# A float32-accurate mixture-of-experts chain on one core: second-layer weights fetched ahead of the float64 conversion and split later, and one vector instruction less per scaling round

## The chip, the cores and the metric

The kernel runs on one core of one Trainium2 chip. The metric is the device time of one execution in microseconds (us); lower is better. A difference of 0.2% here is about 4 us.

## The reference

Three layers follow each other. The first is a windowed attention with global tokens (batch 4, 8 heads, 512 local and 32 global tokens, head size 64); its output x has T = 2176 tokens of 512 numbers. The second, where the change lies, is a mixture of experts in which each token gets a weighted sum of all experts:

```python
P = np.exp(x @ w_gate - max)
for _ in range(8):
    P /= P.sum(1, keepdims=True) + 1e-09
    P /= P.sum(0, keepdims=True) + 1e-09
    P *= N / E
for e in range(E):                       # E = 8
    h = np.maximum(x @ w1[e], 0.0)       # 512 -> 1024
    out += P[:, e:e + 1] * (h @ w2[e])   # 1024 -> 512
```

The third is a dense layer, `elu(x @ w_in) @ w_out`, whose weights (512 x 2048 and 2048 x 512) come as float64.

## The kernel before

**Numbers in two pieces.** TensorE multiplies each matrix as a high and a low piece of 32-bit numbers, three matmuls per product. So each weight that is loaded is "split": ScalarE (ACT) rounds it to the high piece, and VectorE (DVE) or GpSimd (POOL) subtracts that from the weight to get the low piece.

**Phases.** The middle layer is cut into units u = 0 to 15 (half an expert each: 512 hidden columns) and into two sets of tokens, p = 0 (1024 tokens) and p = 1 (1152 tokens). Units 0 and 1 of p = 0 are computed during the attention. The other 30 pairs (p, u) are the phases of the loop at the end of the mixture, numbered a = 0 to 29: a = 0 to 13 have p = 0, a = 14 to 29 have p = 1. A phase has two parts:

- `mix1`: x @ w1, relu, by Strassen's method in its Winograd form. A "quad" (class `Quad`) makes four output blocks from seven products of six matmuls each. A quad's products come in the order 1, 6, 2, 7, 5, 4, and its product 3, which accumulates in the PSUM bank of product 5, comes later, after product 2 of the next quad (for the last quad: in mix2). For p = 0 there are 2 quads of 512 columns, for p = 1 there are 4 quads of 288 columns. Below, "q2.1" is product 1 of the third quad (q0 is the first). ACT copies product 1 out of PSUM (`s`, L834), DVE adds the others to kept sums (`u`, L836, and `t`, L822), ACT makes the relu's high piece (`hh`, L825), DVE the low piece (`hl`, L827).
- `mix2_all`: h @ w2 per tile of 128 tokens (8 tiles for p = 0, 9 for p = 1), 12 matmuls of 512 columns a tile, and DVE adds the result, scaled by P, to the sum (`acc`, L891).

The eight PSUM banks are handed out in turn, so a product or a tile gets the bank of the one eight places before it, and waits until that one has been read.

**Side work.** What else must be done is laid into two lists, `side1` and `side2`, whose items are issued a few at a time after each product of mix1 and each tile of mix2 (function `pop`; `None` is an empty place). All engines run their instructions in the order in which they are issued. The items are:

- `ld1`, `b1` (from `weights1`): two 512 KB loads `w1r` of the next phase's w1 (L669), and 18 items that form and split its Strassen sums (POOL L677, ACT L681, DVE L685).
- `ld2`, `nbuild` (from `weights2`): two 512 KB loads `w2r` of the next phase's w2 (L714), and four items that split it (ACT `w2h` L101, POOL `w2l` L105).
- `cv` (from `weights64`): one or two pieces of the third layer's float64 weights in each phase from a = 2 on (none at a = 13; two at a = 20 to 25): a load `r` of 512 KB (L728), `words` (six DVE instructions, L738 to L743), and `parts` (two on ACT, three on POOL, the last of which makes `cl`, and two stores of 256 KB, L755 and L756, of `ch` and `cl`).
- `plan` (from `sinkhorn`): the eight scaling rounds of P, begun before the loop and ended in phase 0; `cols` is the half of a round that divides by column sums.

All loads and stores are issued by SyncE (SP), in one queue in program order: an issue that waits holds up the ones behind it. The loads `w1r`, `r` and `w2r` share four buffers (`raw_tile`) that are handed out in turn.

Of the kernel before, what the change touches and what calls it, by code (L numbers as in the profile page):

```python
# [16 lines left out]
ALU = mybir.AluOpType  # L17
# [5 lines left out]
T = B * (SL + SG)  # L23
D = H * HD
E, F1 = 8, 1024
F2 = 2048
FU = 512
NT = T // 128
# [20 lines left out]
def tile_net(ctx: ExitStack, tc, kq, vw, vc, qg, wg, w1, w2, wi, wo, consts, out):  # L49
    nc = tc.nc  # L50
# [12 lines left out]
    pr = const.tile([128, NT, E], F32, tag="pr", name="pr")  # L63
# [301 lines left out]
    def put_x(ps, hi, lo):  # L365
        nc.scalar.copy(hi, ps)
        nc.vector.tensor_tensor(out=lo, in0=ps, in1=hi.bitcast(F32), op=ALU.subtract)
# [243 lines left out]
    def raw_tile(shape, dt, name):  # L611
        r = rawm.tile([128, 2 * HALF], F32, tag="raw", name=name)
        n = int(np.prod(shape))
        v = r[:, :n].bitcast(dt)
        return v.rearrange("p (a f) -> p a f", a=shape[0])
# [93 lines left out]
    def weights2(u):  # L709
        v = {}  # L710

        def load(i):
            v[i] = raw_tile((2, 512), F32, "w2r")
            nc.sync.dma_start(v[i], w2[u][:, 2 * i:2 * i + 2])  # L714

        return [lambda: load(0), lambda: load(1)], [
            lambda k=k: split(w2s["h"][:, k], w2s["l"][:, k], v[k // 2][:, k % 2]) for k in range(4)
        ]
# [41 lines left out]
    def sinkhorn():  # L760

        s = {}

        def gmax():
            mx = sm.tile([128, 1], F32, tag="mx", name="mx")
            nc.vector.tensor_reduce(out=mx, in_=lg.rearrange("p t e -> p (t e)"), axis=AX.X, op=ALU.max)
            mb = sm.tile([128, 128], F32, tag="mb", name="mb")
            nc.vector.tensor_copy(mb, mx.to_broadcast([128, 128]))
            s["mb"] = mb

        def expm():
            ps = ps2.tile([128, 512], F32, tag="n", name="pmx")
            nc.tensor.transpose(ps[:, :128], s["mb"], ident)
            nm = sm.tile([128, 1], F32, tag="nm", name="nm")
            nc.vector.tensor_reduce(out=nm, in_=ps[:, :128], axis=AX.X, op=ALU.max, negate=True)
            nc.scalar.activation(
                pr.rearrange("p t e -> p (t e)"), lg.rearrange("p t e -> p (t e)"), AF.Exp, bias=nm
            )

        def rows():  # L780
            r = sm.tile([128, NT], F32, tag="rs", name="rs")
            nc.vector.tensor_reduce(out=r, in_=pr, axis=AX.X, op=ALU.add)
            nc.vector.tensor_scalar_add(r, r, 1e-9)
            nc.vector.reciprocal(r, r)
            nc.vector.tensor_tensor(
                out=pr, in0=pr, in1=r.rearrange("p (t o) -> p t o", o=1).to_broadcast([128, NT, E]), op=ALU.mult
            )
            c = sm.tile([128, E], F32, tag="cs", name="cs")
            nc.vector.tensor_reduce(out=c, in_=pr.rearrange("p t e -> p e t"), axis=AX.X, op=ALU.add)
            s["c"] = c  # L790

        def cols():
            ps = ps2.tile([128, 512], F32, tag="n", name="pcs")
            nc.tensor.matmul(ps[:, :E], ones, s["c"], start=True, stop=True)
            r = sm.tile([128, E], F32, tag="rc", name="rc")
            nc.vector.tensor_scalar_add(r, ps[:, :E], 1e-9)
            nc.vector.reciprocal(r, r)
            nc.vector.tensor_tensor(
                out=pr, in0=pr, in1=r.rearrange("p (o e) -> p o e", o=1).to_broadcast([128, NT, E]), op=ALU.mult
            )  # L800
            nc.vector.tensor_scalar_mul(pr, pr, float(T) / E)

        return [gmax, None, expm] + [rows, None, cols] * 8

# [88 lines left out]
    side1, side2 = deque(), deque()  # L893

    def pop(q, n=1):
        for _ in range(n):
            if q:
                f = q.popleft()
                if f is not None:
                    f()  # L900
# [40 lines left out]
    with tc.manual_schedule():  # L941
        conv = deque(range(8 * U2))
        plan, sums = sinkhorn(), sums_of_x(0, SL)[1]
        first, build = weights1(2)

        pre, plan = deque(sums[:-2] + first + build[:9]), deque(plan)
        steps = 0
        for r in fill:
            steps += 1
            if steps % 4 == 0:  # L950
                pop(pre)
            if steps % 8 == 0:
                pop(plan)
        pop(pre, len(pre))
        for f in build[9:13]:
            f()
        order = [(0, u) for u in range(2, U1)] + [(1, u) for u in range(U1)]
        nload, nbuild = weights2(2)
        side1.extend(build[13:] + sums[-2:] + nload)
        for a, (p, u) in enumerate(order):  # L960
            after = order[a + 1] if a + 1 < len(order) else None
            switch = after is not None and after[0] != p
            if a > 0:
                side1.extendleft(reversed(nbuild))
            else:
                side1.extend(nbuild)
            cv = []
            if after is not None:
                ld1, b1 = weights1(after[1])
                ld2, nbuild = weights2(after[1])  # L970
                side1.extend(ld1)
                if not switch:
                    for _ in range(min(len(conv), 0 if a < 2 else 2 if 19 < a < 26 else 1)):
                        cv.append(weights64(conv.popleft()))
                    side1.extend(ld for ld, _ in cv)
            if a == 0:

                rest, n = list(side1), len(plan)
                side1.clear()
                for b in range(n):  # L980
                    side1.extend(rest[b * len(rest) // n:(b + 1) * len(rest) // n])
                    side1.append(plan.popleft())
            last = mix1(p, u)
            pop(side1, len(side1))
            if after is None:
                break
            if switch:
                ldx, sums = sums_of_x(1, HALF)

                for f in ldx[4:]:  # L990
                    f()
                b1 = ldx[:4] + [f for pair in zip(b1, sums[:12]) for f in pair] + b1[12:] + sums[12:14]
                nbuild = sums[14:] + nbuild
            side2.extend(b1)
            for _, ops in cv:
                side2.extend(ops)
            side2.extend(ld2)
            mix2_all(p, u, last)
            pop(side2, len(side2))
            if switch:  # L1000
                for i in range(TP[0] // 128):
                    nc.sync.dma_start(yd[:, i], accs[i])


        mleft.close()
        fin = ctx.enter_context(tc.tile_pool(name="fin", bufs=1, side="left", reuse_waits="tile"))
        raws = ctx.enter_context(tc.tile_pool(name="raws", bufs=2, side="left", reuse_waits="tile"))
        xh = fin.tile([128, 4, T], F32R, tag="xh", name="xh")
        xl = fin.tile([128, 4, T], F32R, tag="xl", name="xl")
        wset = [{n: fin.tile([128, 4, 512], F32R, tag=s + n, name=s + n) for n in ("1h", "1l")} for s in "AB"]  # L1010

        def x2_t(i, src):
            ps = ps2.tile([128, 4, 128], F32, name="x2t")
            for j in range(4):
                nc.tensor.transpose(ps[:, j, :], src[:, j * 128:(j + 1) * 128], ident)
            c = slice(i * 128, (i + 1) * 128)
            put_x(ps, xh[:, :, c], xl[:, :, c])

        def load_weights(u, ns):
            for n in ns:  # L1020
                nc.sync.dma_start(wset[u % 2][n].bitcast(F32), wd[n][:, u])

        back = {}

        def x_back(j):
            if j == 0:
                load(0)
                load(1)
            for a in range(2):
                x2_t(2 * j + a, back[j][:, a])  # L1030
            if j + 2 < TP[0] // 256:
                load(j + 2)

        def load(j):
            back[j] = raws.tile([128, 2, 512], F32, tag="raw", name="yr")
            nc.sync.dma_start(back[j], yd[:, 2 * j:2 * j + 2])

        side2.extend([None] + [lambda j=j: x_back(j) for j in range(TP[0] // 256)])
        side2.append(lambda: load_weights(0, ("1h", "1l")))
        mix2_all(p, u, last)  # L1040
        pop(side2, len(side2))
# [57 lines left out]
    with tc.manual_schedule():  # L1099
        after = list(range(n0, NT))  # L1100
# [78 lines left out]
```

## Time and profile before

| | |
|---|---|
| median of 3 runs | 2114.24 us (2111.54 to 2114.75) |
| the profiled execution | 2118.01 us, its span 2116.2 us |
| granted TensorE clock, mean over the span | 0.979 |
| PE (TensorE matmul) busy | 2026.4 us, 96% of the span |
| DVE, ACT, POOL busy | 1362.9, 747.0, 710.1 us |
| DMA | 168.45 MB, mean 80 GB/s |

The span is the time from the first to the last instruction of the profiled execution; its own time is 1.8 us longer. A matmul's end is modelled in the profile, so back-to-back matmuls overlap in it, and a stretch in which PE is busy all the time can still differ in speed by the granted clock (1.00 is 2.4 GHz, 0.50 is 1.2 GHz). All rows are of this one execution.

### The profile page before, as it was taken

How to read it: one execution, taken by the hardware profiler on the slowest of the kernel's cores; microseconds unless marked ns; L12 is line 12 of the kernel's file. 1: busy time of each engine (PE TensorE's matmuls, PEld its weight loads, DVE VectorE, ACT ScalarE, POOL GpSimd, SP SyncE). 2: the span in 40 equal slices, each digit the busy share in tenths (PEclk: the TensorE clock that was granted, in tenths of full speed). 3: DMA queues.
4: the chain of work that ended last, by engine and by line, in shares of the span. 5: the costliest groups of instructions: out<-in, count | busy, mean ns of one | idle time of the engine just before them, and what ended most of it. 6: DMA issues, size and time to landing. Idle time of an engine off the chain costs nothing.

```text
span 2116.2 us, 29201 instructions
## 1 busy us (share of the span) xinstructions
PE 2026.4 (96%) x11115; PEld 1768.1 (84%) x11115; DVE 1362.9 (64%) x2534; ACT 747.0 (35%) x1488; POOL 710.1 (34%) x605
## 2 busy tenths in 40 slices
PE   9999979999999999899999988888999999999999
PEld 8998968888888888788888877787888888888897
DVE  7666586676776776766666666666666654444454
ACT  6555424323333332233333322222233333343343
POOL 6545313233333433323322233333332211222222
PEclk9999999999999999999999999999999999999999
DMA  7435221123112211422211222222221140202001
GB/s 229 136 121 175 70 91 60 30 65 114 61 60 97 83 60 68 149 100 82 70 61 60 71 80 80 79 71 71 70 76 64 51 179 1 80 1 80 1 31 55
DMA packets 56444, 168.45 MB, mean 80 GB/s; under 512 B 6128, under 2 KB 7920, under 8 KB 54256
## 3 DMA queue, kind: packets, MB, share of 16 engines
q1 hardware_dynamic: 56304, 166.59, 23.5%
q8 instruction: 87, 1.43, 0.3%
q14 instruction: 53, 0.43, 0.1%
HBM read 138.52 MB, written 28.05 MB: 79 GB/s over the span
## 4 chain that ended last, share of the span: by engine, by line
PE 73%; DVE 10%; ACT 5%; issue 5%; DMA 4%; POOL 2%; SPq 0%; DVEq 0%; ACTq 0%; POOLq 0%
PE m L113 13%; PE m L109 13%; PE m L111 13%; PE q L853 8%; PE q L855 7%; PE q L854 7%; DMA w2r<-in_w_dram 3%; PE o L310 2%; DVE hl L827 2%; DVE eg L130 2%; PE m L1088 1%; PE m L1087 1%; PE m L1090 1%; ACT w2h L101 1%; PE ptp L293 1%
## 5 line engine op out<-in xcount | busy, mean ns | idle before, releaser
L113 PE MATMUL m<-w2h,hl 128*128 128x512 f32 x1088 | 427.0, 392 | 0.0
L109 PE MATMUL m<-w2h,hh 128*128 128x512 f32 x1088 | 426.9, 392 | 0.0
L111 PE MATMUL m<-w2l,hh 128*128 128x512 f32 x1088 | 426.9, 392 | 0.0
L827 DVE SCALAR_TENSOR_TENSOR hl<-t,hh 128x288 fp32r<-128x288 f32 (+1 forms) x368 | 262.9, 714 | 108.5 <-ACT hh L825 103.6
L825 ACT ACTIVATE hh<-t 128x288 fp32r<-128x288 f32 (+1 forms) x368 | 182.1, 500 | 347.8 <-DVE t L822 347.8
L891 DVE SCALAR_TENSOR_TENSOR acc<-m,pr,acc 128x512 f32<-128x512 f32 x247 | 184.3, 749 | 179.6 <-PE m L113 177.9
L105 POOL TENSOR_TENSOR w2l<-w2r,w2h 128x512 fp32r<-128x512 f32 x120 | 171.3, 1457 | 202.2 <-ACT w2h L101 202.2
L113 PEld LDWEIGHTS m<-w2h,hl 128*128 128x128 f32 x1088 | 204.3, 188 | 41.4
L111 PEld LDWEIGHTS m<-w2l,hh 128*128 128x128 f32 x1088 | 204.4, 188 | 40.6
L109 PEld LDWEIGHTS m<-w2h,hh 128*128 128x128 f32 x1088 | 204.4, 188 | 40.1
L822 DVE TENSOR_TENSOR t<-q,u 128x288 f32<-128x288 f32 (+1 forms) x276 | 144.9, 525 | 62.2 <-PE q L855 55.1
L677 POOL TENSOR_TENSOR wt<-w1r 128x512 f32<-128x512 f32 x60 | 78.6, 1311 | 300.1 <-DVE hl L827 251.0
L130 DVE SCALAR_TENSOR_TENSOR eg<-eg,er 128x384 f32<-128x384 f32 (+1 forms) x80 | 77.1, 964 | 148.8 <-ACT er L129 148.8
L677 POOL TENSOR_TENSOR wt<-w1r,wt 128x512 f32<-128x512 f32 x60 | 87.9, 1465 | 234.1 <-DVE wl L685 113.7
L136 POOL TENSOR_SCALAR hh<-eg 128x384 fp32r<-128x384 f32 (+1 forms) x60 | 33.5, 558 | 311.6 <-DVE eg L131 310.5
L681 ACT CAST wh<-wt 128x512 fp32r<-128x512 f32 x120 | 68.8, 619 | 171.4 <-POOL wt L677 171.4
L101 ACT CAST w2h<-w2r 128x512 fp32r<-128x512 f32 x120 | 68.1, 614 | 157.9 <-DMA w2r<-in_w_dram 157.9
L752 POOL TENSOR_TENSOR cp<-r,cp 128x512 f32<-128x512 f32 x32 | 42.0, 1312 | 204.6 <-ACT r L751 204.6
L127 ACT ACTIVATE er<-m 128x384 f32<-128x384 f32 (+1 forms) x80 | 42.8, 535 | 192.0 <-PE m L113 128.3
L853 PE MATMUL q<-x11h,wh 128*128 128x288 f32 (+1 forms) x184 | 62.8, 341 | 34.7 <-DVE t L822 34.7
L685 DVE TENSOR_TENSOR wl<-wt,wh 128x512 fp32r<-128x512 f32 x120 | 88.8, 758 | 0.0
L836 DVE TENSOR_TENSOR u<-q,s 128x288 f32<-128x288 f32 (+1 forms) x92 | 48.4, 526 | 55.0 <-PE q L855 44.0
(268 smaller groups left out, 5066.0 us busy)
## 6 DMA issues: line engine op xcount, KB each, us to landing
w1r<-in_w_dram SPq DMA_DIRECT2D x60, 512.0 KB, 6.7
w2r<-in_w_dram SPq DMA_DIRECT2D x60, 512.0 KB, 5.1
kq<-in_kq_dram SPq DMA_DIRECT2D x31, 544.0 KB, 3.9
r<-in_wi_dram SPq DMA_DIRECT2D x16, 512.0 KB, 4.0
r<-in_wo_dram SPq DMA_DIRECT2D x16, 512.0 KB, 4.0
vw<-in_vw_dram SPq DMA_DIRECT2D x32, 227.5 KB, 4.7
vc<-in_vc_dram SPq DMA_DIRECT2D x8, 568.8 KB, 4.6
raw<-in_w_dram SPq DMA_DIRECT2D x16, 256.0 KB, 5.4
```

The costliest lines, as they stand in the source:

```text
L105: e.tensor_tensor(out=lo, in0=src, in1=hi.bitcast(F32), op=ALU.subtract)
L109: nc.tensor.matmul(ps, ah, bh, start=first, stop=False)
L111: nc.tensor.matmul(ps, ah, bl, start=False, stop=False)
L113: nc.tensor.matmul(ps, al, bh, start=False, stop=last)
L677: eng.tensor_tensor(out=t, in0=get(a), in1=get(b), op=op)
L822: nc.vector.tensor_tensor(out=t, in0=ps, in1=rest, op=ALU.add)
L825: nc.scalar.activation(hh, t, AF.Relu)
L827: late.append(lambda: nc.vector.scalar_tensor_tensor(out=hl, in0=t, scalar=0.0, in1=hh.bitcast(F32), op0=ALU.max, op1=ALU.subtract))
L853: nc.tensor.matmul(ps, wh, xh, start=k == 0 and i != 3, stop=False, skip_group_check=True)
L854: nc.tensor.matmul(ps, wh, xl, start=False, stop=False, skip_group_check=True)
L855: nc.tensor.matmul(ps, wl, xh, start=False, stop=k == 1, skip_group_check=True)
L891: nc.vector.scalar_tensor_tensor(out=accs[i], in0=ps, scalar=scale, in1=accs[i], op0=ALU.mult, op1=ALU.add)
```

## The change

Four edits, all in the mixture's loop but the first:

1. In `cols`, the division by column sums and the factor N / E, two DVE instructions on 128x136 numbers, become one `scalar_tensor_tensor`.
2. In mix2, the loads `ld2` of the next phase's w2 are issued ahead of the float64 pieces' `words` and `parts` instead of behind them.
3. In mix1, the loads `ld1` come first, and the four w2 splits (`nbuild`), which stood first, come after 3 (p = 0) or 8 (p = 1) empty places more; in phase 0 they follow `ld1` directly. The load `r` stays behind them.
4. At the change of p (phase 13), two items of the sums of x that were kept with `nbuild` go to the head of `side1` by themselves, which is where they stood before.

```diff
-            nc.vector.tensor_tensor(
-                out=pr, in0=pr, in1=r.rearrange("p (o e) -> p o e", o=1).to_broadcast([128, NT, E]), op=ALU.mult
+            nc.vector.scalar_tensor_tensor(
+                out=pr, in0=pr, scalar=float(T) / E, in1=r.rearrange("p (o e) -> p o e", o=1).to_broadcast([128, NT, E]),
+                op0=ALU.mult, op1=ALU.mult,
             )
-            nc.vector.tensor_scalar_mul(pr, pr, float(T) / E)
...
-            if a > 0:
-                side1.extendleft(reversed(nbuild))
-            else:
-                side1.extend(nbuild)
             cv = []
             if after is not None:
                 ld1, b1 = weights1(after[1])
+                side1.extend(ld1)
+
+            side1.extend([None] * ((8 if p else 3) if a > 0 else 0) + nbuild)
+            if after is not None:
                 ld2, nbuild = weights2(after[1])
-                side1.extend(ld1)
...
-                nbuild = sums[14:] + nbuild
-            side2.extend(b1)
+                side1.extend(sums[14:])
+            side2.extend(b1 + ld2)
             for _, ops in cv:
                 side2.extend(ops)
-            side2.extend(ld2)
```

**SP's queue, from the loads `r` of the first phase with two float64 pieces (a = 20) on.** Before:

```order
L728 DMA r_11210<-in_wi_dram 128x1024
L728 DMA r_11221<-in_wi_dram 128x1024
L755 DMA wd1h<-ch 128x512
L756 DMA wd1l<-cl 128x512
L755 DMA wd1h<-ch 128x512
L756 DMA wd1l<-cl 128x512
L714 DMA w2r<-in_w_dram 128x1024 x2
L669 DMA w1r<-in_w_dram 128x1024 x2
```

Of the change, at the same place:

```order
L728 DMA r_11281<-in_wi_dram 128x1024
L728 DMA r_11294<-in_wi_dram 128x1024
L714 DMA w2r<-in_w_dram 128x1024 x2
L755 DMA wd1h<-ch 128x512
L756 DMA wd1l<-cl 128x512
L755 DMA wd1h<-ch 128x512
L756 DMA wd1l<-cl 128x512
L669 DMA w1r<-in_w_dram 128x1024 x2
```

The two loads of w2 have moved from behind the four stores to ahead of them; the loads of w1 still follow the stores.

**ACT's queue, from the end of phase 20 into phase 21** (`s` is q0.1's, then q1.1's). Before:

```order
L749 CAST ch<-ct 128x512
L751 ACTIVATE r_11221<-r_11221 128x512
L834 COPY s_11619<-q_11612 128x288
L101 CAST w2h<-w2r 128x512 x2
L825 ACTIVATE hh<-t 128x288
L101 CAST w2h<-w2r 128x512 x2
L825 ACTIVATE hh<-t 128x288 x2
L834 COPY s_11690<-q_11683 128x288
```

Of the change:

```order
L749 CAST ch<-ct 128x512
L751 ACTIVATE r_11294<-r_11294 128x512
L834 COPY s_11611<-q_11604 128x288
L825 ACTIVATE hh<-t 128x288 x3
L834 COPY s_11674<-q_11667 128x288
L825 ACTIVATE hh<-t 128x288 x2
L101 CAST w2h<-w2r 128x512
L825 ACTIVATE hh<-t 128x288
L101 CAST w2h<-w2r 128x512
L825 ACTIVATE hh<-t 128x288
L101 CAST w2h<-w2r 128x512
L834 COPY s_11750<-q_11743 128x288
```

The four casts of w2 stood ahead of the first relu of the phase; now the first of them stands behind five, the fifth being that of q0.3.

**DVE's queue at the end of phase 20** (`acc_105`, `acc_106`, `acc_107` are the last three tiles of mix2). Before:

```order
L743 TENSOR_SCALAR cp<-ct 128x512
L891 SCALAR_TENSOR_TENSOR acc_105<-m_11549,pr,acc_105 128x512
L738 TENSOR_SCALAR ct<-r_11221 128x512
L739 TENSOR_SCALAR ct<-ct 128x512
L740 TENSOR_SCALAR ct<-ct 128x512
L741 TENSOR_SCALAR cp<-r_11221 128x512
L742 TENSOR_TENSOR ct<-ct,cp 128x512
L743 TENSOR_SCALAR cp<-ct 128x512
L891 SCALAR_TENSOR_TENSOR acc_106<-m_11584,pr,acc_106 128x512
```

Of the change:

```order
L743 TENSOR_SCALAR cp<-ct 128x512
L738 TENSOR_SCALAR ct<-r_11294 128x512
L739 TENSOR_SCALAR ct<-ct 128x512
L740 TENSOR_SCALAR ct<-ct 128x512
L741 TENSOR_SCALAR cp<-r_11294 128x512
L742 TENSOR_TENSOR ct<-ct,cp 128x512
L743 TENSOR_SCALAR cp<-ct 128x512
L891 SCALAR_TENSOR_TENSOR acc_106<-m_11576,pr,acc_106 128x512
```

The sum `acc_105` no longer stands between the two pieces' words: it has gone ahead of both, so the first piece's words start one tile later, and the second piece's follow them at once.

## Rows read from the trace of the kernel before

**Rows 1.** The page, busy time by engine: us (share of the span) xinstructions.

```profile
PE 2026.4 (96%) x11115; PEld 1768.1 (84%) x11115; DVE 1362.9 (64%) x2534; ACT 747.0 (35%) x1488; POOL 710.1 (34%) x605
```

**Rows 2.** Waits of PE: us in total, times, longest us.

```profile
PE q L853 <- DVE t L822: 53.8, 21, 6.0
PE pcs L794 <- DVE cs L789: 12.7, 4, 7.1
```

**Rows 3.** Windows: stretch and its length, busy us (instructions), PEclk, DMA share, GB/s.

```profile
884.57:945.27 60.70, 52.51 (x278) 46.92 (x276) 48.79 (x79) 21.31 (x41) 16.18 (x12) 0.89 0.25 83
351.92:843.63 491.71, 491.71 (x2162) 405.46 (x2161) 342.70 (x486) 155.93 (x274) 175.77 (x128) 1.00 0.21 71
945.27:994.12 48.85, 47.05 (x278) 42.56 (x277) 32.38 (x62) 15.29 (x33) 15.02 (x12) 1.00 0.19 66
994.12:1044.59 50.47, 48.57 (x278) 44.08 (x277) 32.69 (x62) 15.37 (x33) 15.04 (x12) 0.97 0.19 63
945.27:1241.94 296.67, 285.57 (x1657) 258.40 (x1656) 195.75 (x374) 91.87 (x198) 90.02 (x67) 0.99 0.20 66
1241.94:1574.51 332.57, 295.15 (x1657) 266.44 (x1656) 223.86 (x407) 98.08 (x210) 114.52 (x85) 0.94 0.22 75
1574.51:1673.87 99.36, 95.64 (x554) 86.65 (x553) 65.01 (x124) 30.55 (x66) 30.13 (x23) 0.98 0.20 64
1673.87:1708.00 34.13, 31.97 (x204) 30.36 (x203) 20.34 (x43) 10.27 (x24) 7.22 (x6) 0.95 0.22 70
```

**Rows 4.** Timeline of PE in phase 21: start us, us, instruction, [idle before <-releaser].

```profile
1252.08 0.29 PE L855 MATMUL q<-x22h,wl 128*128 128x288 f32 x1
1258.22 0.61 PE L853 MATMUL q<-x11h,wh 128*128 128x288 f32 x1 [5.85 <-DVE t L822]
```

**Rows 5.** Timeline of SP's queue at the start of phase 21.

```profile
1250.15 0.32 SPq L756 DMA_DIRECT2D wd1l<-cl  x1
1250.57 0.87 SPq L714 DMA_DIRECT2D w2r<-in_w_dram  x2
```

**Rows 6.** Timeline of ACT at the start of phase 21.

```profile
1246.00 0.38 ACT L834 COPY s<-q 128x288 f32<-128x288 f32 x1
1255.52 1.14 ACT L101 CAST w2h<-w2r 128x512 fp32r<-128x512 f32 x2 [9.14 <-DMA w2r<-in_w_dram]
1256.56 0.44 ACT L825 ACTIVATE hh<-t 128x288 fp32r<-128x288 f32 x1
```

**Rows 7.** Timeline of DVE around the start of phase 21.

```profile
1235.85 0.42 DVE L738 TENSOR_SCALAR ct<-r 128x512 int32<-128x512 int32 x1
...
1238.63 0.74 DVE L891 SCALAR_TENSOR_TENSOR acc<-m,pr,acc 128x512 f32<-128x512 f32 x1
...
1239.74 1.47 DVE L739 TENSOR_SCALAR ct<-ct 128x512 f32<-128x512 f32 x1
...
1245.18 1.40 DVE L891 SCALAR_TENSOR_TENSOR acc<-m,pr,acc 128x512 f32<-128x512 f32 x2
1246.50 0.45 DVE L836 TENSOR_TENSOR u<-q,s 128x288 f32<-128x288 f32 x1
1246.87 0.45 DVE L822 TENSOR_TENSOR t<-q,s 128x288 f32<-128x288 f32 x1
...
1257.04 0.76 DVE L827 SCALAR_TENSOR_TENSOR hl<-t,hh 128x288 fp32r<-128x288 f32 x1 [8.79 <-ACT hh L825]
```

**Rows 8.** Timeline of POOL at the start of phase 21.

```profile
1248.83 1.29 POOL L754 TENSOR_TENSOR cl<-ct,cp 128x512 fp32r<-128x512 f32 x1
1256.21 5.64 POOL L105 TENSOR_TENSOR w2l<-w2r,w2h 128x512 fp32r<-128x512 f32 x4 [6.09 <-ACT w2h L101]
```

**Rows 9.** Lines of DVE, 1002.6 to 1007.9 (first row), 1008 to 1014 (second): busy, mean ns.

```profile
L827 DVE SCALAR_TENSOR_TENSOR hl<-t,hh 128x288 fp32r<-128x288 f32 x4 | 3.7, 917 | 4.2 <-ACT hh L825 4.2
...
L827 DVE SCALAR_TENSOR_TENSOR hl<-t,hh 128x288 fp32r<-128x288 f32 x5 | 2.2, 449 | 0.0
```

**Rows 10.** The factor's line in `cols`: duration ns min/median/max, first and last start.

```profile
L801 DVE TENSOR_SCALAR pr<-pr x8: 230/230/1333, 284.7 to 326.2; 128x136 f32<-128x136 f32 x8
```

## The prediction

> **What bounds the kernel now.** I read the page's busy times first. PE is busy 96% of the span, the others far less [rows 1], so a gain can only come from PE's idle time or from time at the lower clock. The waits of PE name the idle time: 53.8 us in 21 waits of products (L853) for DVE's `t` (L822), that is, for a PSUM bank not yet read; the scaling rounds are a distant second with 12.7 us [rows 2]. The windows by phase say where. Twelve p = 0 phases in a row are busy without a gap at the full clock: 491.71 of 491.71 us, 40.98 each [rows 3]. Each of those has 14 products of 6 and 8 tiles of 12 matmuls, 180 of 512 columns, so one takes 0.228 us. The p = 1 phases are where time is lost. The first in steady state takes 48.85 us of which PE is busy 47.05 at clock 1.00; the last matmul before a gap shows about 0.16 us of modelled end (0.29 shown [rows 4], against (47.05 - 108 x 0.228) / 168 = 0.13 from matmul to matmul). So the floor of a p = 1 phase is 48.85 - 1.80 - 0.16 = 46.9 us. Some of its sisters take 50.47 with the clock at 0.97, and the six from 21 on, which have two float64 pieces beside them, 332.57 / 6 = 55.4 with 0.94 [rows 3].
>
> The cause is seen at the start of phase 21 (1241.94). PE stops at 1252.1 and goes on at 1258.2, released by `t` [rows 4]. DVE had done nothing for 8.79 us before 1257.04: it waited for ACT's `hh` [rows 7]. ACT had done nothing for 9.14 us before 1255.52: its next instruction was a cast of w2, which waited for the load `w2r`, and the relu stood behind it [rows 6]. SP issued that load only at 1250.57, right behind the store of `cl` [rows 5], and POOL had finished `cl` at 1250.12 [rows 8]. So a float64 piece's last step holds up a load in SP's queue, the load holds up ACT, ACT holds up DVE, DVE holds PE's banks, and after a long stop the clock falls as well.
>
> **What the change removes.** The loads of w2 are issued ahead of the pieces, at the fifth of mix2's last eight tiles, some 8 us before the phase ends. Their buffers are free then: with six loads over four buffers the second one takes that of `w1r`'s second half, whose last reader is one of the last two splits at that tile. They land within 5 us (1250.57 to 1255.52, [rows 5, 6]), so before the next phase starts, and ACT's first cast of w2 now stands behind five relus. The chain above is cut at two places.
>
> What it is worth is the excess over 46.9 us [rows 3]. Phases 15 to 20: 296.67 - 6 x 46.89 = 15.3. Phases 21 to 26, each behind or among two pieces: 332.57 - 6 x 46.89 = 51.2. Phases 27 and 28: 99.36 - 2 x 46.89 = 5.6. Phase 29, which has no piece of its own but follows one: 34.13 - 31.97 + 0.16 = 2.3 idle and 5% of 34.13 = 1.7 of clock, 4.0. Together 76.1 us. Phase 14 loses 13.8 (60.70 - 46.9), but its waits are for the sums of x, which the change leaves where they were; I count nothing, and 2 us of gain as the bound, because a cast of w2 stands among its waits too.
>
> **What it adds.** The same work is done later, and two queues tighten.
>
> *Words at the end of a phase.* With two pieces, twelve DVE instructions now follow the third-last tile's sum without a break. The first six took 2.8 us (1235.85 to 1238.63); the sum that stood between them and the second six [rows 7] goes first, so they run from about 1237.4 to 1240.2. The second six took 5.8 us (from that sum's end, 1239.37, to 1245.18), since POOL works beside them: the one at 1239.74 alone took 1.47 us [rows 7], half of all six before. Now they start sooner after the first six, and POOL with the first piece only then, so I take 0.4 us off and get 1245.6. The two last tiles' sums and `u` follow 0.4 us later than before, `u` at 1246.9 instead of 1246.50. From there to the `t` of q0.3 stand eleven instructions, 0.37 us from one to the next where nothing waits (1246.50 to 1246.87), of which one waits for `cl` to end (about 1249.6), and one for ACT's copy behind three relus: I get 1252.7. PE needs that bank at 1252.2, where it stopped before. So 0.5 to 0.6 us of stop remain there.
>
> *Splits in the middle of mix1.* POOL's four subtractions take 5.64 us [rows 8] and now fall on quads q1 and q2. Beside them DVE's `hl` takes 917 ns, beside an idle POOL 449 [rows 9]. A quad has four `hl` and six others at 0.37 us, so with POOL busy it costs DVE 4 x 0.85 + 6 x 0.37 = 5.6 us, and PE gives it 7 x 6 x 0.134 = 5.6. DVE then keeps pace but can't catch up. In phases with one piece it comes into this stretch on time, and the bank that q3.1 needs is read some 0.8 us early: nothing is lost. With two pieces it comes in 0.6 us late, and I book 0.8 us more. So 1.4 us for each of six phases, 8.4 in all. The bounds are 0 and, if PE stops long enough for the clock to fall as it did in 0.97 phases (1.7 us, [rows 3]), some 3 + 1.7 a phase, 28 in all.
>
> Of this overlap the Trainium skill (SBUF — State Buffer, section Who interferes with whom) says that a DVE instruction with two SBUF inputs contends with a GpSimd instruction that reads SBUF, and that the loser fully blocks. The trace agrees as far as `hl` goes (917 against 449 ns). By that rule alone the worst case is a rival below.
>
> *Splits later in p = 0 phases.* They now come after mix1's sixth to ninth product instead of its first four. A product takes 1.37 us, the casts run from about 9.8 us and POOL is done at about 16.2; mix2 starts at 13 x 1.37 = 17.8 and asks for the first and third split first. These phases have no gap today [rows 3] and I expect none. In p = 1 phases POOL is done at 15.7 and mix2 starts at 27 x 0.80 = 21.5.
>
> *Queues.* `w1r` is still behind the stores: issue moves little from where it was, behind the last store's 1250.15 [rows 5], and its first reader comes with mix2, 21 us into the phase. `r` waits for the splits to free its buffer and goes out some 4 us later than before; its reader comes 30 us after. Both are covered. The stores move by up to one tile (2.7 us), and the buffers they read are needed again in q0 and q1 by ACT's copies, which I have at 1250.7 against a release near 1248.3.
>
> *One DVE instruction less in each scaling round.* It occupies 0.23 us [rows 10], so eight are at most 1.8 us of DVE. PE waits for these rounds in four waits [rows 2], and about three of the eight stand in front of one: 0.7 us at most, and I take 0.5, since an instruction's end overlaps the next. The fused instruction has no row of its size. If it took as long as the two it replaces, the gain would be 0; a loss would need it to take longer still, and the fused `hl`, on twice as many numbers, takes 0.45 [rows 9]. In phase 0 the loads of w1 go ahead of the splits: they wait for the same buffer in both orders, so 0.
>
> **Sum.** 2118.0 - 76.1 + 8.4 - 0.5 = 2049.8 for an execution like the profiled one. That one (2118.01) lies 3.8 us over the median of the runs (2114.24), so I take 2046 us, 3.2% less. Best case: no stop left and 2 us from phase 14, 2118.0 - 76.1 - 0.5 - 2 - 3.8 = 2036.
>
> **Rivals.**
>
> *DVE falls behind in the six two-piece phases.* For it: twelve words at a stretch, and POOL busy for nearly all of P to P + 15. Against it: on the whole phase DVE is busy 223.86 of 332.57 us [rows 3]. At the bound above, 28 instead of 8.4, the time is 2066.
>
> *Each `hl` waits for a whole POOL instruction.* Then a quad costs DVE 4 x 1.41 + 6 x 0.37 = 7.9 us against PE's 5.6, 2.3 us lost per quad. Nine one-piece phases lose one quad's worth less their 0.8 us of slack, 1.5, and half of them 1.7 of clock: 21 us. Six two-piece ones lose two quads' worth and the clock: 38. The time is 2046 - 8.4 + 59 = 2097. Against it: the 917 ns of [rows 9] were measured beside just these subtractions. This is what the skill's rule amounts to if DVE always comes second.
>
> *The splits come too late for mix2.* This is the one on the slow side. All 28 phases that split later would stop before mix2. The forecast's gain of 68 us is gone when each stops 68 / 28 = 2.4 us, or 0.7 us with a clock fall of 1.7. In p = 0 that takes POOL's needed splits ending at 18.5 us or later instead of 16.2. At 1.4 us and a fall each, the time is 2046 + 28 x 3.1 = 2133. POOL has no other work there, so I hold it unlikely.
>
> *The wait stays.* If `w2r` still waited (for a buffer that frees late), ACT would wait at P + 9 and the time be 2114. The only late buffer is freed at mix2's fifth tile.
>
> **Chances.** 2036 to 2056: 0.68, and 2046 is the likeliest. The first rival, 2056 to 2076: 0.18. The second, 2076 to 2105: 0.07. The wait stays, within 0.2% (4 us, about what a measurement of this kernel can tell): 0.03. Slower: 0.04. A range from 2034 to 2074 leaves out somewhat under 2 in 10. Faster by over 0.2%: 0.93, the same: 0.03, slower: 0.04.
>
> **What would show it.** Right: `w2r` issued ahead of the stores and no wait of ACT for it; phases 15 to 20 and 27, 28 at 46.9 us with PE busy throughout and clock 1.00; phases 21 to 26 at 48 to 49 with one or two stops of under 1 us, released by `t`; p = 0 phases still at 40.98; `hl` near 0.9 us in the middle of mix1. Wrong: stops of over 2 us in phases 21 to 26 with the clock below 1.00, PE waiting for `w2l` or `w2h` ahead of mix2, or any gap in p = 0 phases. The term most likely to be off is the 8.4 us.

## The result, and the profile after

The changed kernel takes 2045.72 us, the median of three runs (2045.61 to 2048.53), against 2114.24 before: a ratio of 0.968 (95% interval 0.966 to 0.971). The forecast was 2046.0. The profiled execution took 2048.53 us, its span 2046.7, with a mean granted clock of 0.992 (0.979 before).

The page's busy times, as in [rows 1]:

```profile
PE 2006.7 (98%) x11115; PEld 1750.8 (86%) x11115; DVE 1380.7 (67%) x2526; ACT 752.2 (37%) x1488; POOL 701.7 (34%) x605
```

PE issues the same 11115 matmuls and is busy for 20 us less, since fewer of them run at the lower clock. The rest of the gain is idle time. The first three waits of PE, columns as in [rows 2]:

```profile
PE pcs L794 <- DVE cs L789: 11.9, 4, 6.8
PE q L853 <- DVE t L822: 6.3, 7, 1.6
PE q L853 <- ACT xs2h L633: 4.7, 1, 4.7
```

The wait for `t` has gone from 53.8 us in 21 places to 6.3 in 7. The windows of the phases, columns as in [rows 3]: phase 14, the twelve p = 0 phases, phase 15, phases 15 to 20, phases 21 to 26, phases 27 and 28, and phase 29 from its start up to 1642.00. The last one reaches further than that of [rows 3] (223 matmuls against 204), so the two can't be compared by their lengths. A mark that can is the first matmul of the third layer (`x2t`): it comes 30.5 us after the phase's start, and came 34.4 us after it before.

```profile
883.98:945.22 61.24, 52.40 (x277) 46.47 (x276) 48.90 (x79) 21.43 (x41) 14.91 (x11) 0.89 0.30 99
351.33:843.01 491.68, 491.68 (x2162) 405.44 (x2160) 346.90 (x486) 157.46 (x274) 167.11 (x127) 1.00 0.23 73
945.22:992.03 46.81, 46.81 (x278) 42.54 (x276) 33.16 (x62) 15.58 (x33) 14.68 (x12) 1.00 0.21 68
945.22:1226.06 280.84, 280.84 (x1657) 255.21 (x1656) 199.94 (x375) 93.44 (x198) 88.23 (x67) 1.00 0.22 70
1226.06:1514.73 288.67, 283.88 (x1658) 255.64 (x1656) 233.94 (x406) 99.39 (x210) 116.73 (x85) 1.00 0.27 86
1514.73:1608.34 93.61, 93.61 (x553) 85.06 (x552) 66.42 (x124) 31.12 (x66) 29.59 (x23) 1.00 0.21 68
1608.34:1642.00 33.66, 33.66 (x223) 31.72 (x222) 22.42 (x46) 11.41 (x26) 8.58 (x7) 1.00 0.17 48
```

The first two numbers of a row are the stretch and PE's busy time in it. Where they are equal, the profile shows no gap of PE; so it is now in every steady phase but the six with two float64 pieces, and there the clock is 1.00 too. Set against [rows 3], the span's change comes out like this:

| stretch | before, us | after, us | difference | forecast |
|---|---|---|---|---|
| phases 15 to 20 | 296.67 | 280.84 | -15.8 | -15.3 |
| phases 21 to 26 (two pieces) | 332.57 | 288.67 | -43.9 | -51.2 + 8.4 = -42.8 |
| phases 27, 28 | 99.36 | 93.61 | -5.7 | -5.6 |
| phase 29's start to the end of the span | 442.3 | 438.4 | -4.0 | -4.0 |
| phase 14 | 60.70 | 61.24 | +0.5 | 0 |
| phase 0 | 48.82 | 48.29 | -0.5 | -0.5 |
| span | 2116.2 | 2046.7 | -69.5 | -68.2 |

The chain of [rows 5 to 8] can be followed again at phase 21, which starts at 1226.06 (P below). SP's queue:

```profile
1219.51 0.33 SPq L714 DMA_DIRECT2D w2r<-in_w_dram  x1
...
1234.29 0.32 SPq L756 DMA_DIRECT2D wd1l<-cl  x1
1234.71 0.86 SPq L669 DMA_DIRECT2D w1r<-in_w_dram  x2
```

ACT:

```profile
1229.95 0.38 ACT L834 COPY s<-q 128x288 f32<-128x288 f32 x1
...
1232.28 0.45 ACT L825 ACTIVATE hh<-t 128x288 fp32r<-128x288 f32 x1 [1.95 <-DVE t L822]
...
1237.74 0.60 ACT L101 CAST w2h<-w2r 128x512 fp32r<-128x512 f32 x1
```

The first load of w2 went out at 1209.00, 17.1 us ahead of the phase, and the second, once its buffer was free, 6.5 us ahead of it. Before, they went out 8.6 and 9.1 us into it ([rows 5], the row's two issues). The first cast now stands at P + 11.7 and waits for nothing. In these rows ACT waits for DVE alone, under 2 us. DVE:

```profile
1225.53 1.53 DVE L741 TENSOR_SCALAR cp<-r 128x512 int32<-128x512 int32 x1
1227.10 1.67 DVE L742 TENSOR_TENSOR ct<-ct,cp 128x512 int32<-128x512 int32 x1
1228.80 1.40 DVE L743 TENSOR_SCALAR cp<-ct 128x512 int32<-128x512 int32 x1
1230.12 1.40 DVE L891 SCALAR_TENSOR_TENSOR acc<-m,pr,acc 128x512 f32<-128x512 f32 x2
1231.44 0.44 DVE L836 TENSOR_TENSOR u<-q,s 128x288 f32<-128x288 f32 x1
...
1234.50 0.45 DVE L822 TENSOR_TENSOR t<-q,u 128x288 f32<-128x288 f32 x1
...
1236.90 0.45 DVE L822 TENSOR_TENSOR t<-q,u 128x288 f32<-128x288 f32 x1
...
1238.57 1.47 DVE L827 SCALAR_TENSOR_TENSOR hl<-t,hh 128x288 fp32r<-128x288 f32 x1
...
1245.03 0.46 DVE L822 TENSOR_TENSOR t<-q,u 128x288 f32<-128x288 f32 x1
```

Here the two-piece phases still pay: the last words of the second piece hold DVE to P + 5.4, when it makes the first `u`. The three `t` shown are those of q0.4, of q0.3, and of q2.5. PE, in the same phase:

```profile
1236.55 0.30 PE L853 MATMUL q<-x11h,wh 128*128 128x288 f32 x1
...
1244.42 0.29 PE L855 MATMUL q<-x12h,wl 128*128 128x288 f32 x1
1245.55 0.40 PE L853 MATMUL q<-xs4h,wh 128*128 128x288 f32 x1 [0.84 <-DVE t L822]
```

q2.1 starts at 1236.55 without a wait. The phase's one wait in the profile is at q2.3 (1245.55). PE starts there 1.13 us after the matmul before, where 0.13 us is usual, so it stops for 1.0 us (0.7 us in phase 22, 1.0 in the other five): product 3 adds into product 5's bank, and `t` of q2.5, which reads that bank first, only runs at 1245.03.

### The profile page after: what moved, and what is told of

Same layout as the page of the kernel before. It is cut to its first block, busy times and chain, and to the rows that moved or that the text cites. A ratio compares the mean times of both kernels' runs of the same rounds, so it can differ in the third digit from the quotient of the medians.

```text
span 2046.7 us, 29207 instructions
## 1 busy us (share of the span) xinstructions
PE 2006.7 (98%) x11115; PEld 1750.8 (86%) x11115; DVE 1380.7 (67%) x2526; ACT 752.2 (37%) x1488; POOL 701.7 (34%) x605
## 5 line engine op out<-in xcount | busy, mean ns | idle before, releaser
L827 DVE SCALAR_TENSOR_TENSOR hl<-t,hh 128x288 fp32r<-128x288 f32 (+1 forms) x368 | 286.5, 778 | 3.9 <-ACT hh L825 0.6
L105 POOL TENSOR_TENSOR w2l<-w2r,w2h 128x512 fp32r<-128x512 f32 x120 | 160.6, 1355 | 237.2 <-ACT w2h L101 220.6
L127 ACT ACTIVATE er<-m 128x384 f32<-128x384 f32 (+1 forms) x80 | 42.8, 535 | 192.2 <-PE m L113 128.5
L749 ACT CAST ch<-ct 128x512 fp32r<-128x512 f32 x32 | 19.9, 623 | 202.0 <-DVE ct L742 202.0
L251 ACT ACTIVATE e<-s,m 128x192 f32<-128x192 f32 (+1 forms) x128 | 55.5, 435 | 59.5 <-DVE m L243 58.9
```

The source lines that it names most:

```text
L105: e.tensor_tensor(out=lo, in0=src, in1=hi.bitcast(F32), op=ALU.subtract)
L827: late.append(lambda: nc.vector.scalar_tensor_tensor(out=hl, in0=t, scalar=0.0, in1=hh.bitcast(F32), op0=ALU.max, op1=ALU.subtract))
```

## The experiments

Eight runs were made, in two sets of four, each set on one chip; in each set the kernel before ran beside them, with a median of 2112.19 us (13 runs, 2106.87 to 2114.61) and of 2112.68 us (7 runs, 2109.62 to 2114.93). Ratios are to those. All of them compute the whole reference.

### The early loads alone

The kernel before with this edit and no other; the splits stay at the head of mix1.

```diff
-            side2.extend(b1)
+            side2.extend(b1 + ld2)
             for _, ops in cv:
                 side2.extend(ops)
-            side2.extend(ld2)
```

> The kernel before with the w2 loads issued ahead of the float64 pieces, and nothing else changed (splits at the head of mix1, two instructions in each scaling round). Theory, the load was the wait: the casts stand first but find their data, so phases 15 to 20, 27, 28 fall to 46.8 us as in the changed kernel; in phases 21 to 26 POOL's splits follow its conversion at once, DVE has POOL beside it from 0 to 14 us of the phase, and they take about 49.5 instead of 48.1. Time about 2055 (2048 to 2065). Rival, the place of the splits was the wait: the phases stay at 48.7 and 55.4, time 2105 to 2114.

Measured: 2048.09 us (2046.97 to 2049.16), ratio 0.970 (0.968 to 0.971). Windows of phases 15 to 20 and 21 to 26:

```profile
943.73:1224.57 280.84, 280.84 (x1658) 255.21 (x1656) 198.48 (x375) 93.08 (x198) 88.76 (x67) 1.00 0.21 70
1224.57:1513.48 288.91, 283.58 (x1658) 255.53 (x1657) 230.91 (x406) 98.83 (x210) 118.68 (x85) 1.00 0.26 86
```

POOL's splits, and the one stop of phase 21, which starts at 1224.57:

```profile
1232.74 5.88 POOL L105 TENSOR_TENSOR w2l<-w2r,w2h 128x512 fp32r<-128x512 f32 x4
```

```profile
1238.49 0.40 PE L853 MATMUL q<-xs4h,wh 128*128 128x288 f32 x1 [0.87 <-DVE t L822]
```

This one edit is worth nearly the whole gain. The one-piece phases are at the floor, the two-piece ones at 48.11 to 48.19. The splits come at P + 8.2, right behind `cl`, and the stop moves ahead with them, from q2.3 to q1.3. I had expected more to be left behind.

### The later splits alone

The changed kernel with the loads put back behind the pieces and the scaling rounds as before (the lines of the rounds are left out here).

```diff
...
-            side2.extend(b1 + ld2)
+            side2.extend(b1)
             for _, ops in cv:
                 side2.extend(ops)
+            side2.extend(ld2)
```

> The kernel before with the splits 3 or 8 places later and the w1 loads first, but the w2 loads still behind the float64 stores and two instructions in each scaling round. Theory: with one piece the load has landed 7 us into the phase and the first cast stands at 9 to 10, so phases 15 to 20, 27, 28 fall to 46.8; with two it lands at 13.6, ACT waits some 3 us, PE stops about 3 us at q3.1 and the clock falls, phases 21 to 26 take about 51.5. Time about 2066 (2058 to 2076). Rival, the load alone was the wait: nothing gained in one-piece phases either, over 2100.

Measured: 2049.14 us (2047.75 to 2050.18), ratio 0.970 (0.969 to 0.972); a miss by 17 us. Windows, as above, and then ACT and DVE in the first two-piece phase (which starts at 1225.02):

```profile
944.18:1225.02 280.84, 280.84 (x1657) 255.21 (x1656) 200.84 (x374) 93.40 (x198) 88.15 (x67) 1.00 0.21 70
1225.02:1516.32 291.30, 282.52 (x1658) 255.43 (x1656) 228.59 (x407) 98.78 (x210) 115.71 (x85) 1.00 0.26 86
```

```profile
1238.46 0.62 ACT L101 CAST w2h<-w2r 128x512 fp32r<-128x512 f32 x1 [2.92 <-DMA w2r<-in_w_dram]
```

```profile
1239.46 1.32 DVE L827 SCALAR_TENSOR_TENSOR hl<-t,hh 128x288 fp32r<-128x288 f32 x1 [2.36 <-ACT hh L825]
```

The load is as late as I expected, ACT waits for it 2.9 us, and DVE waits for ACT 2.4 us. But PE stops for only 1.4 to 1.9 us a phase, and the clock stays at 1.00. The five relus ahead of the cast let DVE read the banks of q0 and q1 before it is held up, so most of ACT's wait is slack by then. In the one-piece phases ACT doesn't wait for the load at all: that wait occurs 6 times in the whole trace (18.6 us), against 28 times (157.9 us) before.

So the two moves are not two halves of the gain. Each cuts the chain by itself, one by bringing the load forward, the other by letting the relus go ahead of the cast.

### The scaling round alone

The kernel before with the fused instruction of edit 1 and nothing else.

> The kernel before with only the two DVE instructions of each scaling round made one. Theory: PE's waits for the column sums fall from 12.7 to about 11.9 us and phase 0 from 48.8 to 48.3, nothing else moves; time 2113.5, not to be told from before by the clock on the wall. Rival: the fused instruction takes as long as both and phase 0 stays at 48.8.

Measured: 2110.56 us (10 runs, 2106.31 to 2114.85), ratio 0.9995 (0.998 to 1.0005), no difference that can be told. The trace shows what it does: phase 0 takes 48.29 us instead of 48.82, and the waits of PE for the rounds are 11.9 us instead of 12.7, with the wait for `t` still there:

```profile
PE q L853 <- DVE t L822: 51.7, 21, 5.9
PE pcs L794 <- DVE cs L789: 11.9, 4, 6.8
```

### Double pieces in p = 0 phases

The changed kernel with the six double pieces moved from phases 20 to 25 to phases 5 to 10.

```diff
-                    for _ in range(min(len(conv), 0 if a < 2 else 2 if 19 < a < 26 else 1)):
+                    for _ in range(min(len(conv), 0 if a < 2 else 2 if 4 < a < 11 else 1)):
```

> The changed kernel with the six phases that convert two float64 pieces moved from a = 20 to 25 (p = 1) to a = 5 to 10 (p = 0). Theory, the last 1.3 us of phases 21 to 26 come from DVE's backlog behind twelve words and POOL: all p = 1 phases from 15 on take 46.8, and p = 0 phases, which have DVE busy 70% and a bank slack of 8 products of 1.37 us, stay at 40.97; time 2045.7 - 6 x 1.3 = 2038. Rival, the p = 0 phases have no room for a second piece: some of phases 6 to 11 stop by over 1.3 us, time 2046 or more.

Measured: 2039.6 us (2037.39 to 2042.06), ratio 0.966 (0.964 to 0.967). Every p = 0 phase takes 40.97 us and every p = 1 phase from 15 on 46.81. It ran again in the second set beside the changed kernel:

> The changed kernel with two float64 pieces in phases 5 to 10 instead of 20 to 25, beside the changed kernel on one chip. Expected 8 us (0.4%) less than the changed kernel, all p = 1 phases from 15 on at 46.8. Rival: the difference of the first look was one of chips, and both take the same.

> The changed kernel itself once more, as the measure for the runs beside it on the same chip. Expected: 0.968 of before, phases 21 to 26 at 48.1 us, all other p = 1 phases from 15 on at 46.8.

Measured: 2038.85 us (2038.56 to 2039.25), ratio 0.965 (0.964 to 0.966), against 2047.51 (2045.84 to 2049.43), ratio 0.969 (0.968 to 0.971), for the changed kernel. This version beats both kernels, the changed one by 8.7 us. Its first waits of PE:

```profile
PE pcs L794 <- DVE cs L789: 11.9, 4, 6.8
PE q L853 <- ACT xs2h L633: 4.7, 1, 4.7
PE m L109 <- ACT hh L133: 2.2, 7, 0.6
```

The wait for `t` is gone from the top. So what the change left in phases 21 to 26 belongs to the second piece, and p = 0 phases have room for it.

### Splits later still in p = 1

What makes the remaining stop: DVE's late start alone, the splits beside mix1 alone, or both? The changed kernel with 14 empty places for 8 moves the splits to the end of mix1.

```diff
-            side1.extend([None] * ((8 if p else 3) if a > 0 else 0) + nbuild)
+            side1.extend([None] * ((14 if p else 3) if a > 0 else 0) + nbuild)
```

> The changed kernel with the w2 splits of p = 1 phases behind 14 empty places instead of 8, six products later. Theory, the 1.3 us of phases 21 to 26 are the sum of DVE's late start behind the words and of its slow pace beside the splits: with POOL idle six products longer DVE catches up first (1.9 us per quad), and the stop at q2.3 goes, phases 46.8 to 47.3. Rival one, the late start alone makes the stop: it stays at 1.0 us. Rival two, the splits are now too late for mix2: every p = 1 phase stops before its first tile, over 47.5 us also with one piece.

Measured: 2039.78 us (2039.03 to 2040.35), ratio 0.965 (0.964 to 0.967). Window of phases 21 to 26, and POOL in phase 21, which starts at 1223.99:

```profile
1223.99:1506.40 282.41, 282.38 (x1658) 255.57 (x1657) 233.34 (x406) 98.81 (x210) 117.89 (x85) 1.00 0.27 88
```

```profile
1240.74 5.72 POOL L105 TENSOR_TENSOR w2l<-w2r,w2h 128x512 fp32r<-128x512 f32 x4 [8.54 <-ACT w2h L101]
```

DVE makes its first `u` at P + 5.4, as late as in the changed kernel, yet no stop remains, and the six phases are 6.3 us shorter. They take 47.1 us each, 0.3 us over the floor, though PE shows no gap in them; what makes up this rest is not shown. With the splits at P + 16.7 DVE has caught up before POOL gets in its way. With one piece the splits beside q1 and q2 cost nothing (46.81). So it takes both: a late start, and the slow stretch before it is made up.

### Splits too late in p = 0

The forecast's slow rival, put to the test: as many empty places in p = 0 as in p = 1, and one item of `side1` after each product (else the longer list would be taken two at a time, and the splits would not move as far).

```diff
-        per = -(-len(side1) // (len(steps) - 2))
+        per = -(-len(side1) // (len(steps) - 2)) if u == 2 and p == 0 else 1
...
-            side1.extend([None] * ((8 if p else 3) if a > 0 else 0) + nbuild)
+            side1.extend([None] * ((8 if p else 8) if a > 0 else 0) + nbuild)
```

> The changed kernel with the w2 splits of p = 0 phases behind 8 empty places instead of 3 (one item after each product, the fourth split and the load behind mix1's last product). Theory, POOL's third split now ends about 21 us into the phase and mix2 asks for it at 18.7: each of the 13 phases stops 2 us or more and the clock falls in some, 43 to 45 us a phase, time 2075 to 2100. Rival: mix2 is not held up by the splits, phases stay at 40.97 and the time at 2046.

Measured: 2087.7 us (one run). Window of phases 1 to 13, then PE's waits, then POOL and PE at the end of one mix1:

```profile
349.15:925.31 576.16, 543.76 (x2342) 441.44 (x2340) 368.04 (x515) 168.99 (x291) 192.09 (x138) 0.99 0.23 73
```

```profile
PE m L109 <- ACT w2h L101: 16.4, 13, 1.3
PE m L111 <- POOL w2l L105: 16.0, 13, 1.7
```

```profile
409.52 1.29 POOL L105 TENSOR_TENSOR w2l<-w2r,w2h 128x512 fp32r<-128x512 f32 x1 [23.75 <-ACT w2h L101]
412.24 3.45 POOL L105 TENSOR_TENSOR w2l<-w2r,w2h 128x512 fp32r<-128x512 f32 x2 [1.43 <-ACT w2h L101]
```

```profile
413.58 0.49 PE L109 MATMUL m<-w2h,hh 128*128 128x512 f32 x1 [1.31 <-ACT w2h L101]
...
415.75 0.50 PE L111 MATMUL m<-w2l,hh 128*128 128x512 f32 x1 [1.68 <-POOL w2l L105]
```

Mix2 stops twice in each of these 13 phases, first for a high piece of w2 and then for a low one. Ten of them take 43.9 to 44.5 us, and three take 45.3, in which the clock falls for a while (0.96 on the mean of the phase at 526.00). They lose 576.16 - 13 x 40.97 = 43.5 us together, 3.3 each. The mechanism of that rival is real; with three empty places the change stays short of its point. In the changed kernel POOL's last splits of phase 8, which starts at 638.14, are these:

```profile
648.50 3.80 POOL L105 TENSOR_TENSOR w2l<-w2r,w2h 128x512 fp32r<-128x512 f32 x3 [7.25 <-ACT w2h L101]
652.57 1.43 POOL L105 TENSOR_TENSOR w2l<-w2r,w2h 128x512 fp32r<-128x512 f32 x1 [0.28 <-ACT w2h L101]
```

They end at P + 15.9, and mix2 starts at P + 17.7 (655.88).

## Why the prediction was right, and where it was not

**The chain and its price.** Shown. With the load ahead of the pieces ACT's wait for it is gone, and so is DVE's long wait for `hh`. The second load went out 6.5 us ahead of the phase, where the forecast had some 8 for both, which was early enough. The floor taken from one phase of before, 46.9 us, is 46.81, and the terms of 15.3, 5.6 and 4.0 us came out at 15.8, 5.7 and 4.0.

**"The chain above is cut at two places."** True, but the forecast didn't say that one cut is enough. The two kernels with one move each stand within 4 us of the changed one.

**The 8.4 us for two-piece phases.** The size was nearly right (6 x (48.11 - 46.81) = 7.8), the place wrong. The step that failed is "PE needs that bank at 1252.2, where it stopped before", which had q2.1 wait for `t` of q0.3 and then q3.1 for a later one. After the change that `t` comes at P + 10.8 (1236.90), just when it was forecast (1252.7 is P + 10.8 of before), and PE doesn't wait for it: q2.1 starts at 1236.55, ahead of it. It needs the bank that `t` of q0.4 (1234.50) reads. The trace of before showed this already. Behind the `hl` of 1257.04 [rows 7] DVE's next two `t` of the form `t<-q,u` are those of q0.4 and of q0.3:

```profile
1257.72 0.45 DVE L822 TENSOR_TENSOR t<-q,u 128x288 f32<-128x288 f32 x1
...
1260.63 0.45 DVE L822 TENSOR_TENSOR t<-q,u 128x288 f32<-128x288 f32 x1
```

PE goes on at 1258.22 [rows 4], just after the first of them and ahead of the second. So a product does not always get the bank of the one eight places before it. What the two traces fit is banks handed out in the order in which they come free: q0.5's comes free only after q0.3. The first due time that DVE misses is q2.3's, in a bank of its own quad. There one stop of about 1.0 us stands, and about 0.3 us of slightly slower matmuls make up the rest.

Two sizes behind that step were off as well. `u` of q0.6 came at P + 5.4, not P + 5.0: the 0.4 us that I took off the second piece's words did not come off, since three of them again took 1.40 to 1.67 us beside POOL. DVE's `hl` beside the splits took 1115 ns (mean of the four from 1238.5 to 1243.9), not 917 [rows 9]; in the one-piece phases it was near 1.07 us (1066 ns in phase 15), where the forecast's sign had 0.9. These sizes were too small and the due time too early, which act in opposite directions, so that 7.8 stands so near to 8.4 is luck.

**DVE falls behind (2066).** It does come late in those six phases, but with the stops of up to 1.0 us the clock stayed at 1.00, and the loss is 7.8 us of the 28 this rival had. Where the pieces are moved, none of it is left, and where the splits are moved no stop and 1.6 us in all (282.41 - 6 x 46.81).

**Each `hl` waits for a whole POOL instruction (2097).** Not so here. The Trainium skill (SBUF — State Buffer, section Who interferes with whom) says that a DVE instruction with two SBUF inputs contends with a GpSimd one that reads SBUF, and that the ports they share are under an exclusive lock. The four `hl` beside the splits agree as far as they are held up, two of them by 0.7 us and one, of 1.47 us, by a little over 1 us. Their mean of 1.12 us lies between the 0.92 that I took and this rival's 1.41. The one-piece phases, which this rival charged with 21 us, lost nothing.

**Splits too late (2133).** Not reached, as shown above. Its price of 3.1 us a phase is close to the 3.3 that the p = 0 phases paid when it was made to happen, but it was made up otherwise: a stop of 1.4 us and a fall of the clock in each there, two stops in each and a fall in three of 13 here.

**Scaling rounds, phase 14, the median.** The fused instruction takes 0.30 us, as the plain one had, and phase 0 gained 0.5 us as forecast. Phase 14 lost 0.5 us where I counted nothing (61.24 us, and 61.00 when the changed kernel ran again, against 60.70); no experiment took up why. The profiled execution was forecast at 2049.8 and took 2048.5, and it lay 2.8 us over its median instead of 3.8. The two errors, of 1.3 and 1.0 us, cancel.

## What to carry to other kernels

When an engine waits long for another one that looks idle, follow the second one's own queue: here a load issued behind a store that waited for POOL held up a cast, and the cast held up relus on which PE's banks depended, so the cure was an order on SP or on ACT and not a faster engine. Price a repair by what one undisturbed phase of the same kind takes, and test each part alone before adding the parts up, since two cuts in one chain pay once. And find the due time of a buffer from what the trace shows releasing the waiting instruction, not from a rule on how buffers are handed out.

## What the runs showed of the hardware that was not expected

DVE's integer instructions are slowed by POOL too, and not only those with two inputs. In [rows 7] a word at 1235.85 takes 0.42 us, with POOL idle; in phase 21 after the change, `cp<-r`, with one input, took 1.53 us beside these of POOL:

```profile
1225.26 1.52 POOL L752 TENSOR_TENSOR cp<-r,cp 128x512 f32<-128x512 f32 x1 [9.22 <-ACT r L751]
1226.74 1.47 POOL L753 TENSOR_TENSOR ct<-ct,ch 128x512 f32<-128x512 f32 x1
1228.29 1.63 POOL L754 TENSOR_TENSOR cl<-ct,cp 128x512 fp32r<-128x512 f32 x1
```

It and the two words after it, at 1227.10 and 1228.80, each end 0.3 to 0.6 us after the end of one of these. POOL's own three took 1.47 to 1.63 us there, against 1.29 with less beside them [rows 8]. Which property of these words makes them contend, no run here tells.

The clock was less sensitive to short stops than [rows 3] made me think: PE stops of 0.7 to 1.9 us in each of six phases, in three kernels (the changed one, the early loads alone, the later splits alone), went with a granted clock of 1.00 throughout, where an idle time of 1.8 to 1.9 us a phase before had gone with 1.00 in one phase and 0.97 in its sister. Two waits close together, of 1.3 and 1.7 us, went with a lower clock in three of the 13 phases that had them (splits too late in p = 0).
